# A spectral layer beside a routed expert layer: the inverse row transform on f32, and work between the engines dealt out anew

## The chip, the cores and the metric

The kernel runs on one core of one Trainium2 chip. The metric is the device time of one launch in microseconds; the whole kernel is one launch. A time comes with the span of the profile, from the core's first instruction to its last, which is some 2 us shorter.

## The reference

The input is normalised row by row; two layers work on the result, and both are added to the input. Cut to what matters:

```python
S, D = 2048, 576            # rows, columns
x  = A_x
xn = layernorm(x)           # no learned scale
# A: a filter in the frequency plane
X = rfft2(xn) * (w_r + 1j * w_i)        # 2048 x 289
a = irfft2(X, (S, D))
# B: for each row and each of 32 heads, one expert of 64
q  = einsum("nd,dhc->nhc", xn, w_q)     # c = 2 * 128
s1 = q[..., :128] @ k1.T                # 8 scores
s2 = q[..., 128:] @ k2.T                # 8 scores
e  = 8 * argmax(s1) + argmax(s2)        # the softmax over one candidate is 1
b  = sum over heads of gelu(xn . u[e]) * v[e]
out = x + a + b
```

## The kernel before, in words

**Layer A** is a two-dimensional Fourier transform made of matrix products. The 2048 rows are 16 tiles of 128. `ln` takes mean and variance of some tiles; the standard deviation's inverse lies in `rr[:, 0]`, and `rr[:, 2]` is -4 times the mean. `folds(t)` adds and subtracts mirrored halves of a row tile, twice, so that a transform of 576 needs short products; the result is `F`, and `Rs` is the first transform's matrix scaled by the row's `rr`. `dft128(t)` multiplies them: a transform over 64 rows. Its result lies in `AB` as f32 (a view, `AF_`) and in `ABL` (33 leftover frequencies, as f16 high and low halves). For three of the 16 tiles (`RTS`) the products are cut into halves of 64 array rows.

Then 16 steps `g` each hold 128 rows of the frequency plane: `d_fwd(g)` is the forward row transform on f32 (products named `c,AB`), `s_fwd` the column transform, `s_mul` multiplies with the filter (`Wt`), `s_inv` is the inverse column transform. `s_inv` writes its result back into `AB`, as an f16 high half (ScalarE) and an f16 low half, the difference (VectorE). Last come the 16 row tiles `t`: `d_inv(t)` is the inverse row transform, three f16 products (high by high, high by low, low by high) for each of four pieces, an eviction with the inverse scale `sc[:, 12:13]`, and folds on VectorE and GpSimd; `fin(t)` turns the result back over 64 rows with the matrix `RT`, adds layer B's products with `v` in the same PSUM bank, adds the input and stores.

**Layer B** never makes `q`: the keys are folded into `w_q` (`fold_part`, `fold_end`, `fold_last`), as differences from the first key of eight, so that each of the 64 (head, side) pairs has 7 score columns of 448 in `MU` and `MUL`; 64 more columns are `u`. `x_t` loads the transposed input and splits it into two f16 halves. `scores(r)` (8 times, 256 rows each) multiplies them: 28 products of 512 columns each, named `MU,xT` and `MUL,xT`. After it VectorE finds the maximum over a pair's 7 columns (`mx`), flags who equals it (`w<-banks,mx`) and weights the flags with a power of two of the key's number (`w<-w,wt`). `route(r)` reduces these to an expert's code and `combine(r)` to the 64 experts' weights, which GpSimd and TensorE turn (`CZ`) for `fin`.

**The order.** The program is first recorded as a list of operations, with their dependencies. `issue` then runs a planner (`forward`): a model of the five engines that takes, whenever an engine is free, the ready operation with the best place in the table `RANK`. So the table and the model's costs set the order on every engine, and which PSUM banks are used. Each engine works its list in order. All instructions come out of one helper line, so the profile is read by the names of tiles.

Of the kernel before, what the change touches and what calls it, by code (L numbers as in the profile page):

```python
# [32 lines left out]
def _consts():  # L33
# [13 lines left out]
    place = np.arange(16).reshape(4, 4).T.ravel()  # L47
# [48 lines left out]
    C1[[0, 144, 288]] *= 0.5  # L96
    C1 = np.where((j <= 144)[:, None] == ev[None, :], C1, 0)
# [12 lines left out]
    ic = np.zeros((128, 2, 2, 290), np.float16)  # L110
# [6 lines left out]
    for b, m in enumerate((_clean(CI) * 64, _clean(SI) * 64)):  # L117
        hi, lo = _hl(m)
        for q, h in enumerate((hi, lo)):
            ce = slice(0, 145) if b == 0 else slice(145, 290)  # L120
            co = slice(145, 290) if b == 0 else slice(0, 145)
            ic[:, b, q, ce] = h[:128, ce]
            ic[:, b, q, co] = h[161:, co]
        il[:99, b] = np.concatenate([hi[128:161], hi[128:161], lo[128:161]])
    c16 = np.concatenate([dl.reshape(128, -1), ic.reshape(128, -1), il.reshape(128, -1)], 1)
    c16 = np.concatenate([dc.reshape(128, -1), c16.view(np.float32)], 1)
# [164 lines left out]
class _Plan:  # L291
# [7 lines left out]
    def cost(self, eng, m, out, ins, kw):  # L299
# [6 lines left out]
        if eng == "tensor":  # L306
# [3 lines left out]
            if kw.get("tile_position"):  # L310
                q = _parts(ins[0])
                return c * q[0] * q[1] / 16384, 230.0
# [222 lines left out]
def _body(ctx, tc, nc, plan, a, out):  # L535
# [366 lines left out]


    XT, gate = {}, set()

    @staged
    def x_t(r):

# [343 lines left out]
```

## Time and profile before

| | |
|---|---|
| time of the runs, us | 223.46, 222.16, 222.97; median 222.97 |
| the profiled execution: time, span | 221.33 us, 219.5 us |
| busy, us | PE 193.5, DVE 178.0, ACT 132.5, POOL 134.1 |
| granted TensorE clock | 0.995 |
| read, written | 43.0 MB, 4.7 MB |

PE is TensorE's products, PEld its weight loads, DVE VectorE, ACT ScalarE, POOL GpSimd. A row of a group gives its line, engine, operation, what it writes and reads, shapes and number of instructions; then the busy time in us and the mean duration in ns; then the idle time of the engine just before them and what ended it. The ends of products are modelled; their starts are not, so a product's price is the distance between starts. A product on f32 leaves two records.

### The profile page before, as it was taken

To read this page: it belongs to the slowest core of one execution; us is meant where nothing else is said; L and a number is where in the kernel's file an instruction comes from. 1 tells how busy PE (TensorE), PEld (TensorE's weight loads), DVE (VectorE), ACT (ScalarE), POOL (GpSimd) and SP (SyncE) were. 2 spreads that over 40 slices of the span, in tenths; PEclk is the share of its full clock that TensorE was granted. 3 is DMA by queue.
4 is the path that set the end of the run, shared out by engine and by line. 5 is a ranking of instruction groups with operands and counts; after the bars stand their busy time and mean duration, and the time that the engine had idled before them with its cause. 6 is when DMAs were issued, how large, how long until landed. Compare 5 with 4: busy or idle time off the path is not lost.

```text
span 219.5 us, 6058 instructions
## 1 busy us (share of the span) xinstructions
PE 193.5 (88%) x2360; PEld 130.7 (60%) x2360; DVE 178.0 (81%) x417; ACT 132.5 (60%) x285; POOL 134.1 (61%) x179
## 2 busy tenths in 40 slices
PE   0197899999999989999989999999979999998690
PEld 0175576679568546764657545655547787477560
DVE  1989899854646777763999999998899999999980
ACT  2268787979946977988595983855832333043220
POOL 4776787515189307394767963947734985667560
PEclk9999999999999999999999999999999999999998
DMA  6999999999999999993362404201100136204376
GB/s 198 380 417 418 422 418 423 395 403 400 366 383 356 405 408 423 437 345 133 103 199 63 131 0 122 73 3 24 39 0 3 28 87 162 54 0 108 96 176 165
DMA packets 17020, 48.12 MB, mean 219 GB/s; under 512 B 2144, under 2 KB 8544, under 8 KB 16224
## 3 DMA queue, kind: packets, MB, share of 16 engines
q1 hardware_dynamic: 16992, 47.74, 60.6%
q8 instruction: 18, 0.29, 0.5%
q14 instruction: 10, 0.08, 0.1%
HBM read 43.01 MB, written 4.72 MB: 217 GB/s over the span
## 4 chain that ended last, share of the span: by engine, by line
PE 50%; DVE 33%; ACT 6%; issue 5%; DMA 2%; POOL 1%; ACTq 0%; DVEq 0%; POOLq 0%
PE banks L523 50%; DVE MT L523 8%; DVE t L523 7%; DVE w L523 5%; DVE XN L523 3%; DVE AB L523 2%; DVE mx L523 2%; DVE st L523 2%; DMA XN<-in_x_dram 2%; DVE A L523 2%; DVE ABL L523 2%; ACT t L523 1%; ACT ABL L523 1%; ACT AB L523 1%; ACT Rs L523 1%
## 5 line engine op out<-in xcount | busy, mean ns | idle before, releaser
L523 PE MATMUL banks<-MU,xT 128*128 128x512 f16 x192 | 45.5, 379 | 0.4 <-DVE t L523 0.4
L523 POOL TENSOR_TENSOR A<-t 128x145 f32<-128x145 f32 (+2 forms) x48 | 32.3, 688 | 14.1 <-DVE t L523 11.6
L523 PE MATMUL banks<-c,AB 128*128 128x145 f16 (+2 forms) x320 | 38.2, 253 | 1.0 <-DVE AB L523 1.0
L523 POOL TENSOR_TENSOR y<-t,t 128x289 f32<-128x289 f32 x32 | 23.0, 742 | 20.9 <-DVE t L523 20.5
L523 PEld LDWEIGHTS <-xT 128*128 128x128 f16 x224 | 20.9, 98 | 23.9 <-issue 0.9
L523 POOL TENSOR_TENSOR xT<-xf,xT 128x640 f16<-128x640 f32 x16 | 22.4, 1403 | 18.2 <-ACT xf L523 18.1
L523 DVE SCALAR_TENSOR_TENSOR t<-banks,wx,Wt 128x578 f32<-128x578 f32 x32 | 24.4, 810 | 4.1 <-PE banks L523 4.0
L523 ACT ACTIVATE yh<-banks,sc 128x580 f32<-128x580 f32 (+1 forms) x16 | 10.0, 627 | 25.1 <-PE banks L523 24.0
L523 POOL TENSOR_TENSOR yh<-y,yh 128x578 f16<-128x578 f32 x16 | 21.8, 1377 | 4.7 <-issue 2.7
L523 ACT ACTIVATE AB<-banks 128x512 f32<-128x512 f32 (+1 forms) x32 | 18.7, 592 | 5.5 <-PE banks L523 2.9
L523 PE MATMUL banks<-Rs,yl 128*99 128x128 f32 (+1 forms) x76 | 10.3, 290 | 12.6 <-ACT Rs L523 12.1
L523 PE MATMUL banks<-w,KP 128*32 128x288 f32 x256 | 20.4, 420 | 0.6 <-DMA w<-in_wq_dram 0.4
L523 PE MATMUL banks<-c,ABL 99*128 99x289 f16 (+1 forms) x64 | 18.6, 295 | 2.4 <-DVE XN L523 1.4
L523 DVE TENSOR_TENSOR ABL<-banks,ABL 33x256 f16<-33x256 f32 x32 | 12.9, 407 | 8.8 <-ACT ABL L523 6.2
L523 POOL TENSOR_TENSOR t<-XN 128x289 f32<-128x289 f32 x20 | 15.8, 799 | 5.3 <-DMA XN<-in_x_dram 2.5
L523 PEld LDWEIGHTS banks<-c,AB 128*128 128x128 f32 x128 | 18.0, 191 | 1.5 <-DVE AB L523 0.9
L523 PEld LDWEIGHTS <-AB 128*128 128x128 f16 x192 | 17.2, 146 | 2.5 <-issue 1.6
L523 PE MATMUL banks<-Rs,A 128*128 128x128 f32 (+1 forms) x152 | 18.0, 291 | 0.4 <-ACT Rs L523 0.4
L523 DVE TENSOR_REDUCE MT<-w 128x128 bf16<-128x896 bf16 (+1 forms) x16 | 18.3, 1141 | 0.1
L523 PEld LDWEIGHTS banks<-Rs,A 128*128 128x128 f32 (+1 forms) x152 | 16.8, 205 | 2.0 <-ACT Rs L523 1.0
L523 PE MATMUL banks<-A,s 64*64 64x289 f32 x256 | 17.8, 410 | 0.0
L523 PEld LDWEIGHTS banks<-Rs,yl 128*99 128x99 f32 (+1 forms) x76 | 8.1, 177 | 15.8 <-ACT Rs L523 13.5
(126 smaller groups left out, 409.1 us busy)
## 6 DMA issues: line engine op xcount, KB each, us to landing
w<-in_wq_dram SPq DMA_DIRECT2D x32, 576.0 KB, 7.4
xf<-in_xT_dram SPq DMA_DIRECT2D x16, 320.0 KB, 3.9
Wt<-in_W_dram SPq DMA_DIRECT2D x8, 578.0 KB, 6.9
out_dram<-XN SPq DMA_DIRECT2D x32, 144.0 KB, 2.4
XN<-in_x_dram SPq DMA_DIRECT2D x3, 1154.0 KB, 10.2
s<-in_s_dram SPq DMA_DIRECT2D x16, 192.0 KB, 4.2
XN<-in_xd_dram SPq DMA_DIRECT2D x2, 1152.0 KB, 8.9
XN<-in_xd_dram SPq DMA_DIRECT2D x1, 2304.0 KB, 12.9
```

The costliest lines, as they stand in the source:

```text
L523: fn(*[x.place() if isinstance(x, _Ps) else x for x in args], **{k: x.place() if isinstance(x, _Ps) else x for k, x in kw.items()})
```

## The change

- The inverse row transform takes f32: `s_inv` writes one f32 result with ScalarE, VectorE's subtraction of 512 elements falls away, `d_inv` has one f32 product in the place of three f16 ones, and the constants `ic` are f32 (as many bytes).
- The inverse scale goes into the last transform's constants: `RT` is multiplied with it once. The evictions of `d_inv` then have no pointer to a scale, and VectorE's are plain adds and subtracts. In the same way `cst` takes the scale of `combine`.
- The score columns lie key by key (64 pairs for each of 7 keys) instead of pair by pair. The flags of score tiles 0 to 6 are weighted by seven ScalarE instructions of 128 elements each, and `combine`'s two casts to integers go to ScalarE.
- A constant column is zeroed in the forward constants, so the folds need no mean: a plain add takes the place of the one with `rr[:, 2]`, and the step that made it goes.
- Of the second folds, GpSimd gives eight to VectorE (`DF`). Of the 16 input splits, six (`XL`) go from ScalarE and GpSimd to one VectorE instruction each.
- `RTS` goes: all 16 first transforms are whole. The table that turns the Gelu on is loaded by an instruction of its own (`gelu_table`).
- The planner's costs differ, and `RANK` is another table.

```diff
-    1200, 1203, 1204, 1217, 1230, 1244, 1205, 1236, 588, 595, 828, 589, 1117, 799, 1029, 1035, 319, 1118, 965,
+    769, 771, 812, 1250, 1253, 1279, 757, 802, 305, 871, 417, 306, 842, 1217, 951, 1061, 935, 1086, 981, 983,
...
+    C1[:, ll == 0] = 0.0
...
-        for q, h in enumerate((hi, lo)):
...
-            ic[:, b, q, ce] = h[:128, ce]
-            ic[:, b, q, co] = h[161:, co]
+        ic[:, b, ce] = m[:128, ce]
+        ic[:, b, co] = m[161:, co]
...
-ABt = AB.rearrange("p q c (n t) -> p q c n t", t=16)
+ABt = AF_.rearrange("p c (n t) -> p c n t", t=16)
...
-    RTS = (9,10,11,)
+    DF = (0,2,4,6,8,10,12,14,)
...
-        G.tensor_tensor(F[:, 1, 0:145], e[:, 1, 0:145], e[:, 1, 288:143:-1], op=OP.add)
-        V.scalar_tensor_tensor(F[:, 0, 0:145], e[:, 0, 0:145], rr[:, 2, t:t + 1], e[:, 0, 288:143:-1],
-                               op0=OP.add, op1=OP.add)
+        (V if t in DF else G).tensor_tensor(F[:, 1, 0:145], e[:, 1, 0:145], e[:, 1, 288:143:-1], op=OP.add)
+        V.tensor_tensor(F[:, 0, 0:145], e[:, 0, 0:145], e[:, 0, 288:143:-1], op=OP.add)
...
+        V.tensor_scalar(RT, RT, sc[:, 12:13], None, op0=OP.mult)
...
+            if 2 * r + i in XL:
+                V.scalar_tensor_tensor(v, w, bx[:, 3:4], h, op0=OP.mult, op1=OP.subtract)
+                continue
...
-        V.tensor_tensor(wk[:, 896:1792].rearrange("p (t n) -> p t n", t=2), wk[:, 0:896].rearrange("p (t n) -> p t n", t=2),
-                        wt.unsqueeze(1).to_broadcast([128, 2, 448]), op=OP.mult)
+        if r in AW:
+            for e in range(7):
+                A.activation(we[:, :, e], eq[:, :, e], AF.Copy, scale=2.0 ** -(6 * e + 6 + 6 * (e > 2)))
+        else:
+            V.tensor_tensor(we, eq, wt.unsqueeze(1).to_broadcast([128, 2, 7, 64]), op=OP.mult)
...
-            V.tensor_scalar(ci[:, :, w], cw[:, w].rearrange("p t i -> p (t i)"), 2.0 ** (18 + 30 * w), None, op0=OP.mult)
+            A.activation(ci[:, :, w], cw[:, w].rearrange("p t i -> p (t i)"), AF.Copy, scale=2.0 ** (18 + 30 * w))
...
-        A.activation(hi, pv, AF.Copy)
-        V.tensor_tensor(ab, pv, hi, op=OP.subtract)
+        A.activation(ABz[:, :, z, :], pv, AF.Copy)
...
-                for n, (ha, hb) in enumerate(((0, 0), (0, 1), (1, 0))):
-                    P.matmul(p[:, b, cs], ABt[:, ha, 2 * c + b, :, t], ic[:, b, hb, cs], start=False,
-                             stop=(c == 1 and n == 2))
+                P.matmul(p[:, b, cs], ABt[:, 2 * c + b, :, t], ic[:, b, cs], start=False, stop=(c == 1))
...
-        V.scalar_tensor_tensor(eo[:, :, 0:145], p[:, :, 0:145], sc[:, 12:13], qs, op0=OP.mult, op1=OP.add)
+        V.tensor_tensor(eo[:, :, 0:145], p[:, :, 0:145], qs, op=OP.add)
```

Three places of the order. The first is VectorE where the inverse row transforms are under way and the last score tile (`mx_130`, `w_123`) comes; `XN` is the addition to the input of one finished row tile, `t` an eviction of `d_inv`, `MT` are the small tiles of `route` and `combine`. Before:

```order
L523 SCALAR_TENSOR_TENSOR t_1_99<-banks,sc,yh_134 128x2x145
L523 TENSOR_REDUCE MT<-w_122 128x32
L523 SCALAR_TENSOR_TENSOR MT<-MT,sc 128x128
L523 TENSOR_REDUCE mx_130<-banks 128x128
L523 TENSOR_TENSOR MT<-MT,fm 128x128
L523 TENSOR_TENSOR w_123<-banks,mx_130 128x896
L523 SCALAR_TENSOR_TENSOR XN<-banks,sc,XN 128x576
L523 SCALAR_TENSOR_TENSOR t_0_98<-banks,sc,yh_133 128x2x145
L523 TENSOR_TENSOR w_123<-w_123,wt 128x896
L523 SCALAR_TENSOR_TENSOR MT<-MT,sc 128x128
L523 SCALAR_TENSOR_TENSOR t_1_99<-banks,sc,yh_134 128x2x144
L523 SCALAR_TENSOR_TENSOR t_1_99<-banks,sc,yh_134 128x2x145
```

Now:

```order
L527 TENSOR_REDUCE mx_130<-banks 128x128
L527 TENSOR_TENSOR t_0_98<-banks,yh_133 128x2x145
L527 SCALAR_TENSOR_TENSOR XN<-banks,sc,XN 128x576
L527 TENSOR_TENSOR w_123<-banks,mx_130 128x896
L527 SCALAR_TENSOR_TENSOR XN<-banks,sc,XN 128x576
L527 TENSOR_TENSOR w_123<-w_123,wt 128x896
L527 TENSOR_TENSOR t_1_99<-banks,yh_134 128x2x145
L527 TENSOR_TENSOR t_1_99<-banks,yh_134 128x2x144
L527 TENSOR_REDUCE MT<-w_123 128x128
L527 TENSOR_TENSOR t_0_98<-banks,yh_133 128x2x145
L527 SCALAR_TENSOR_TENSOR XN<-banks,sc,XN 128x576
L527 SCALAR_TENSOR_TENSOR MT<-mx_130,MT 128x128
```

Before, six of the 16 row tiles' additions stand ahead of the last score tile's maximum (five of them above these rows), and now none: the score tiles have moved ahead of the inverse row transforms.

The second place is ScalarE in the score tiles, where it evicts PSUM (`A<-banks` is `d_fwd`, `AB<-banks` is `s_inv`), splits the input (`xT`, `xf`) and takes Gelus (`MT<-banks,gs`). Before:

```order
L523 ACTIVATE xf_124<-xf_124,bx 128x640
L523 ACTIVATE MT<-banks,gs 128x64
L523 ACTIVATE xT_94<-xf_125,bx 128x640
L523 ACTIVATE xf_125<-xf_125,bx 128x640
L523 ACTIVATE AB<-banks 128x8x64
L523 ACTIVATE ABL<-banks 99x4x64
L523 ACTIVATE t_0_108,wm<-Wt_112 128x1156
```

Now:

```order
L527 ACTIVATE yl_106<-yh_133 128x396
L527 ACTIVATE xT_94<-xf_125,bx 128x640
L527 ACTIVATE w_121<-w_121 128x2x64 x7
L527 ACTIVATE xT_95<-xf_126,bx 128x640
L527 ACTIVATE MT<-banks,gs 128x64
L527 ACTIVATE A_1_101<-banks 128x578
L527 ACTIVATE xT_95<-xf_124,bx 128x640
L527 ACTIVATE MT<-MT 128x16
```

Seven weightings of one score tile's flags stand in a row ahead of the next eviction; a copy `xf` is gone, since VectorE splits that tile, and a cast to integers has come.

The third place is the start of the queue of loads on SP: `XN` are the blocks of x, `c_68` the first constants, `w` the weights of the fold, `s` and `Wt` column matrices and filter. Before:

```order
L523 DMA XN<-in_x_dram 128x1154
L523 DMA s_1_116<-in_s_dram 128x384
L523 DMA s_3_118<-in_s_dram 128x384
L523 DMA c_68<-in_c_dram 128x320
L523 DMA XN<-in_x_dram 128x1154
L523 DMA kT<-in_kT_dram 128x16
L523 DMA s_2_117<-in_s_dram 128x384
L523 DMA s_0_115<-in_s_dram 128x384
L523 DMA XN<-in_x_dram 128x2308
L523 DMA w_119<-in_wq_dram 128x1152
L523 DMA XN<-in_x_dram 128x2308
```

Now:

```order
L527 DMA kT<-in_kT_dram 128x16
L527 DMA XN<-in_x_dram 128x1154
L527 DMA c_68<-in_c_dram 128x320
L527 DMA mk<-in_mk_dram 128x99
L527 DMA XN<-in_x_dram 128x1154
L527 DMA s_0_115<-in_s_dram 128x384
L527 DMA XN<-in_x_dram 128x2308
L527 DMA w_120<-in_wq_dram 128x1152
L527 DMA Wt_112<-in_W_dram 128x1156
L527 DMA XN<-in_x_dram 128x2308
```

The constants `s` that stood between the blocks of x have moved behind, the small `kT` has moved to the front, and a filter block stands ahead of the last block but one.

More of the change, by code (lines that the diff above doesn't have):

```diff
@@ L45, in _consts @@
     R = _clean(R)
-    place = np.arange(16).reshape(4, 4).T.ravel()
+    place = np.arange(16) // 2 + 8 * (np.arange(16) % 2)
     F = np.zeros((2, 64, 16, 2, 2, 2))
@@ L757, in dft128 @@
         for b in range(2):
-            P.matmul(p[:99, 1, 128 * b:128 * b + 128].rearrange("p (q i x) -> p i q x", i=2, x=8), FL[:, b, :, :].rearrange("p a b -> p (a b)"), Rs, start=True, stop=True)
-        A.activation(hi, m, AF.Copy)
+            P.matmul(p[:99, 1, 128 * b:128 * b + 128], FL[:, b, :, :].rearrange("p a b -> p (a b)"), Rs, start=True, stop=True)
+        A.activation(AF_.rearrange("p c (h n) -> p (c h) n", n=64)[:, :, 4 * t:4 * t + 4], m, AF.Copy)
+        lo = ABL[:99].rearrange("p b (h n) -> p (b h) n", n=64)[:, :, 4 * t:4 * t + 4]
         A.activation(lo, l, AF.Copy)
@@ L895, in fold_last @@
             turned(p[:, c], c, 3)
-        m = MU[:, :, :, 336:448].rearrange("p h c (m e) -> p h c m e", e=7)
-        parted(m[:, 0], m[:, 1], p[:, :, :, :7], 1)
+        m = MU[:, :, :, :448].rearrange("p h c (e m) -> p h c e m", m=64)[:, :, :, :, 48:64]
+        q = p.rearrange("p c m e -> p c e m")[:, :, :7]
+        A.activation(m[:, 0], q, AF.Copy, scale=sc[:, 7:8])
+        for c in range(4):
+            V.scalar_tensor_tensor(m[:, 1, c], q[:, c], sc[:, 7:8], m[:, 0, c], op0=OP.mult, op1=OP.subtract)
         p = PS("m", (128, 16, 8))
         turned(p, 4, 3)
-        m = MUL[:, :, 336:448].rearrange("p h (m e) -> p h m e", e=7)
-        parted(m[:, 0], m[:, 1], p[:, :, :7], 1, 64)
+        m = MUL[:, :, :448].rearrange("p h (e m) -> p h e m", m=64)[:, :, :, 48:64]
+        parted(m[:, 0], m[:, 1], p.rearrange("p m e -> p e m")[:, :7], 1, 64)
     XT, gate = {}, set()
+    XL = (4,5,6,7,8,9,)
     @staged
@@ L1005, in d_fwd @@
                 cs = slice(0, 145) if b == c else slice(145, 289)
-                P.matmul(p[:, b, cs], ABg[:, 2 * b + c, g // 4, g % 4, :], dc[:, b, cs], start=False, stop=(c == 1))
+                P.matmul(p[:, b, cs], ABg[:, 2 * b + c, g // 2, g % 2, :], dc[:, b, cs], start=False, stop=(c == 1))
         A2[g] = T([128, 2, L], F32, "A2", 2)
@@ L1099, in d_inv @@
             es = T([128, 2, 290], F32, "qs", 2, "yh")
-            A.activation(es, p[:, :, 0:290], AF.Copy, scale=sc[:, 12:13])
+            A.activation(es, p[:, :, 0:290], AF.Copy)
             qs = es[:, :, 145:290]
```

98 lines of the change are left out of this document (43 added, 55 removed), and 124 rows, old and new, of the table RANK.

## The prediction

> **What bounds the kernel now.** I read first the busy time of the engines by stage. I cut the span where the work changes kind: loading; layer norm, folds and the first transform; the column transforms with the weights being folded; the same with the scores; the inverse row transforms and the output; the last store. The numbers are the stage's length, then busy time (and instructions) of PE, PEld, DVE, ACT and POOL, the granted clock, the DMA share and the rate.
>
> ```profile
> 0.00:10.00 10.00, 0.05 (x1) 0.05 (x1) 5.47 (x24) 2.74 (x6) 5.55 (x17) 1.00 0.81 273
> 10.00:49.60 39.60, 36.04 (x358) 27.39 (x358) 33.93 (x115) 31.23 (x85) 25.66 (x44) 1.00 1.02 415
> 49.60:103.20 53.60, 52.60 (x676) 35.38 (x676) 32.38 (x80) 43.67 (x85) 28.61 (x30) 1.00 0.96 373
> 103.20:163.70 60.50, 58.75 (x691) 34.11 (x688) 56.41 (x103) 40.13 (x79) 40.82 (x42) 1.00 0.24 69
> 163.70:213.70 50.00, 46.05 (x644) 33.80 (x644) 49.05 (x98) 14.70 (x33) 33.48 (x48) 1.00 0.32 77
> 213.70:219.50 5.80, 0.00 (x0) 0.00 (x0) 0.79 (x1) 0.00 (x0) 0.00 (x0) 0.82 0.71 170
> ```
>
> From 10 us on, TensorE idles 3.56, 1.00, 1.75 and 3.95 us in the four working stages. VectorE fills the last of them to 49.05 of 50.00 us, and the one before to 56.41 of 60.50. So two engines are full at once, TensorE throughout and VectorE from 103 us on. The chain of waits agrees: long stretches on TensorE alone, and VectorE for the rest.
>
> ```profile
> PE 50%; DVE 33%; ACT 6%; issue 5%; DMA 2%; POOL 1%; ACTq 0%; DVEq 0%; POOLq 0%
> ```
>
> ```profile
> 78.34 30.53 PE banks L523 x374
> ```
>
> Then I asked what TensorE waits for: first in the inverse stage, then in the first-transform stage (total us, times, longest; the 10.0 of the last row is the wait for the very first input).
>
> ```profile
> PE banks L523 <- DVE XN L523: 2.0, 4, 1.1
> PE banks L523 <- DVE t L523: 1.1, 2, 0.7
> PE banks L523 <- DVE ABL L523: 0.9, 1, 0.9
> PE banks L523 <- DVE AB L523: 0.5, 1, 0.5
> PE banks L523 <- POOL A L523: 0.2, 1, 0.2
> ...
> PE banks L523 <- ACT Rs L523: 12.6, 4, 10.0
> ```
>
> In the inverse stage all waits but 0.2 us are for VectorE. That is what the change relieves. It cannot return more than TensorE now waits, and whatever it adds to TensorE is paid in full.
>
> **The change part by part.** *Inverse row transform on f32.* Per row tile and half, two products on f32 replace six on f16. Their prices are read from starts, since the ends are modelled; the forward transform already has the f32 shape.
>
> ```profile
> 85.50 0.66 PE L523 MATMUL banks<-c,AB 128*128 128x145 f32 x4
> 85.99 0.29 PE L523 MATMUL banks<-c,ABL 99*128 99x289 f16 x1
> 86.12 0.66 PE L523 MATMUL banks<-c,AB 128*128 128x144 f32 x4
> 86.70 0.45 PE L523 MATMUL banks<-w,KP 128*32 128x288 f32 x4
> ...
> 192.39 0.56 PE L523 MATMUL banks<-c,AB 128*128 128x145 f16 x6
> 192.79 0.29 PE L523 MATMUL banks<-c,ABL 99*128 99x290 f16 x1
> ```
>
> Four f32 records, two products, take 85.50 to 85.99, or 0.245 us a product. Six f16 products take 192.39 to 192.79, or 0.067 each, and three of them 0.20. So the 64 products cost TensorE 64 x (0.245 - 0.20) = +2.9 us, with nothing to hide them. Between 86.12 and 86.70 lie 0.58 us for four records, 0.09 more than above: the price of a change of the array's shape. The new order has 102 such changes for 98, +0.4 us. The three row-tiled first transforms that go cost about what the plain ones cost: 0. TensorE: +3.3 us.
>
> The inverse weights are read with a step of 16 elements, 64 bytes on f32, and no f32 load here has a step. The nearest rows are the f16 load with a step and the f32 load without.
>
> ```profile
> L523 PEld LDWEIGHTS <-AB 128*128 128x128 f16 x192 | 17.2, 146 | 2.5 <-issue 1.6 <-DVE AB L523 0.6
> L523 PEld LDWEIGHTS banks<-c,AB 128*128 128x128 f32 x128 | 18.0, 191 | 1.5 <-DVE AB L523 0.9
> ```
>
> Stepped loads of 146 ns already start every 67 ns, so 79 ns of one lie under its neighbour. An f32 load of 191 less 79 needs 112 ns, under the 122 ns of an f32 record: hidden, +0. If the step makes it half as long again (287), it needs some 208 and shows by 86 ns on 128 loads: +11 us. I take 0, since the f32 row is the nearer one, and keep 11 as the end.
>
> Of a load of 128 columns the Trainium skill (TensorE: Matmul & The Clock Gate, LDWEIGHTS) says that it takes the columns over 1.2 GHz, 107 ns, an estimate by which it would stay hidden as well. The page says nothing there of a step, and no run here shows a stepped f32 load.
>
> *VectorE in the inverse stage.* Its rows in that stage, and the score products that TensorE runs there:
>
> ```profile
> L523 DVE TENSOR_REDUCE MT<-w 128x32 f32<-128x1024 bf16 x5 | 6.0, 1206 | 0.0
> L523 DVE TENSOR_TENSOR w<-w,MT 128x512 bf16<-128x512 bf16 x10 | 4.6, 485 | 0.0
> L523 DVE TENSOR_SCALAR MT<-MT 128x16 int32<-128x16 f32 x10 | 2.4, 263 | 0.0
> L523 DVE TENSOR_REDUCE mx<-banks 128x128 f32<-128x896 f32 x2 | 2.1, 1074 | 0.0
> L523 DVE TENSOR_TENSOR w<-banks,mx 128x896 bf16<-128x896 f32 x2 | 2.1, 1074 | 0.0
> L523 DVE TENSOR_TENSOR w<-w,wt 128x896 bf16<-128x896 bf16 x3 | 1.9, 624 | 0.0
> ...
> L523 PE MATMUL banks<-MU,xT 128*128 128x512 f16 x36 | 8.6, 379 | 0.4 <-DVE t L523 0.4
> ```
>
> In the new order two of these five sums are left there, four of the ten products, none of the ten integer casts (ScalarE has them), one maximum and one comparison of two, and one weighting of three: 3.6 + 2.8 + 2.4 + 1.1 + 1.1 + 1.2 = 12.2 us. The smaller pieces of the same score tiles give some 3 more. The 24 evictions without a pointer to a scale give 24 x 0.06 = 1.5: the row with it is 506 ns, and the plain reads of PSUM below (407 for 256 elements, 678 for 512) put 290 elements at 443. VectorE falls from 49 to about 32 us. Most of this is moved, not saved: 36 of the 44 score products, some 8 us of TensorE, now stand ahead of the first inverse transform. TensorE needs 46.05 - 8 + 3.3 = 41.4 us here, so VectorE has 9 us to spare and the wait for it should mostly go. I take -3.0 of 3.95. Ends: -3.95, and 0 if other waits fill the room.
>
> *VectorE before that.* All 16 subtractions of the column transform's result go, seven of eight weightings, and six input splits come to it. The rows for these and for the terms further down:
>
> ```profile
> L523 DVE TENSOR_TENSOR AB<-banks,AB 128x512 f16<-128x512 f32 x16 | 10.8, 678 | 2.0 <-ACT AB L523 2.0
> L523 DVE TENSOR_TENSOR ABL<-banks,ABL 33x256 f16<-33x256 f32 x32 | 12.9, 407 | 8.8 <-ACT ABL L523 6.2 <-ACT AB L523 2.6
> L523 DVE SCALAR_TENSOR_TENSOR t<-banks,sc,yh 128x290 f32<-128x290 f32 x16 | 8.1, 506 | 0.0
> L523 DVE SCALAR_TENSOR_TENSOR A<-t,rr 128x145 f32<-128x145 f32 x16 | 7.1, 448 | 0.9 <-POOL t L523 0.7
> L523 DVE TENSOR_TENSOR A<-t 128x288 f32<-128x288 f32 x16 | 7.2, 448 | 0.0
> L523 DVE SCALAR_TENSOR_TENSOR vS<-Wt,sc,vS 128x576 f16<-128x576 f32 x1 | 0.8, 819 | 0.3 <-ACT vS L523 0.3
> L523 POOL TENSOR_TENSOR A<-t 128x145 f32<-128x145 f32 x16 | 8.5, 535 | 6.3 <-DVE t L523 4.1 <-PE banks L523 1.0 <-ACT Rs L523 0.9
> L523 POOL TENSOR_TENSOR xT<-xf,xT 128x640 f16<-128x640 f32 x16 | 22.4, 1403 | 18.2 <-ACT xf L523 18.1
> L523 ACT ACTIVATE xf<-xf,bx 128x640 f32<-128x640 f32 x16 | 13.2, 823 | 0.2
> L523 ACT ACTIVATE CZ<-MT 128x128 f16<-128x128 f32 x8 | 2.5, 308 | 5.6 <-DVE MT L523 5.6
> ```
>
> In the score stage VectorE loses nine subtractions (6.1), its weightings (3.1) and casts (1.6); it gains what was moved forward (some 12.3) and three splits (near the 819 row, 0.9 each: 2.7). That is 56.4 + 4.2, or 61 of a stage that grows to 68 us. TensorE waits 1.75 us there, and I leave that: 0, between -1.75 and +3. The column stage idles 1.0 us; without the subtraction between eviction and next use, -0.3.
>
> *ScalarE.* 49 weightings of 128 elements, near the 308 ns row, are 15.1 us, and 16 small casts some 4; six of the 823 ns copies go, 4.9, and GpSimd is relieved of six splits of 1403 ns. In the score stage ScalarE comes to 40.1 + 15 + 3 - 2.5 = 56 of 68 us. It has room, so I cost this at 0. But it evicts PSUM in the same queue: up to 2.2 us of weightings, seven in a row, can stand ahead of an eviction that TensorE waits for. That is a rival below.
>
> A rule of the Trainium skill speaks against this part: ScalarE: Activation LUTs, Rules for kernel authors, has multiplication on VectorE, up to three times faster in bf16. The trace agrees on the price, 624 ns for one weighting against 7 x 308 = 2156; by this rule the change loses wherever ScalarE is waited for.
>
> *First transform.* The mean is no longer folded in, so 16 fused adds of 448 ns become plain adds. The row with 288 plain elements is 448, and its share for 145 is 226; I take 300, so -2.4 us. Eight folds come from GpSimd, +2.4. VectorE: 0 (ends -3.5 and 0). GpSimd loses 8 x 0.535 = 4.3 us of 25.66, and the step that scaled the mean. The loads are reordered: ahead of the end of the second and third block of x stand 1.40 and 2.78 MB for 1.74 and 3.32. At the stage's 415 GB/s they land 0.8 and 1.3 us earlier; the first block, behind a load of 8 KB, hardly later. TensorE idles 3.56 us here, 2.6 of it for Rs, which comes after that chain. I take -2.0 (ends -3.56 and +0.5).
>
> **Sum:** +3.3 - 3.0 - 0.3 - 2.0 = -2.0 us. The profiled execution took 221.33 us, 219.5 of span and 1.8 around it, so 219.3. The median of the runs is 222.97, 1.6 above that execution, and on its scale I predict 221.0. The bound between change and none is 0.5%, 1.1 us, about what a measurement of this kernel can tell.
>
> **The rivals**, on the median's scale.
>
> *The waits go altogether.* TensorE's idle time of all four stages, 10.26 us, shrinks to 3: +3.3 - 7.3 = -4.0, and 1 us of waits shorter than a matmul's modelled end comes on top: 218. With all of it gone and that 1 us: 215.0. For it: VectorE, which most waits name, is relieved. Against it: in the first-transform stage, where much of the idle time lies, VectorE has as much work as before.
>
> *Slower: the filler is gone.* In the inverse stage before, score products filled TensorE while a tile went from its transform through ScalarE, VectorE and GpSimd to the last product. Now 8 of 44 are left, and GpSimd, 33.48 us of 50 before, has the same work in 42, 80%. If its adds become the last thing waited for, the stage idles 7 us in place of 3.95: +3.3 + 3 - 0.3 - 1.5 = +4.5, or 227.5. It decides as soon as the inverse stage gives back less than 1 us: already then +3.3 - 1 - 1 makes 224.3. For it: TensorE has the least room of all engines. Against it: only 0.2 us of today's waits name GpSimd.
>
> *ScalarE comes late.* If half of the seven weighting blocks each hold an eviction for 2.2 us, +7.7 on the forecast: 228.7. For it: 56 of 68 us are taken. Against it: no wait of TensorE in that stage names ScalarE today. The rule of ScalarE: Activation LUTs named above points this way.
>
> *The stepped f32 load shows:* +11 at most, 232; half of it, 226.5.
>
> **How the numbers follow.** Forecast (219 to 223.5) 0.46; waits gone 0.18; filler gone 0.21; ScalarE late 0.08; load 0.07. Faster by over 0.5%, below 221.9: 0.18 and three quarters of 0.46, together 0.52. Same: 0.10 of the forecast and 0.04 of the filler's mild end, 0.14. Slower: 0.34. Below 215.5 I leave some 0.04, above 228 some 0.14, of the last two rivals and the worst of the filler. The likeliest case's own range is 219 to 223.5.
>
> **What would show it.** Right: 128 f32 records of the inverse at a pitch near 122 ns; no subtraction named AB; VectorE under 36 us and TensorE's idle time under 1.5 in the inverse stage, which is 41 to 43 us long; a score stage near 68; the first-transform stage near 37.6. Wrong: a pitch over 140 (load); waits of TensorE for GpSimd of over 1 us in the inverse stage (filler); waits for ScalarE of over 2 us in the score stage; a first-transform stage no shorter than 39.6, which takes the 2.0 away and leaves the time near 223.

## The result, and the profile after

The changed kernel takes 237.62 us, median of 4 runs (237.20 to 238.09), beside 222.56 for the kernel before (4 runs, 221.69 to 223.46): a ratio of 1.068, 95% interval 1.062 to 1.073. It is slower by 15 us, and outside the predicted range. The profiled execution took 238.09 us with a span of 236.3, 16.8 more span than before.

The busy time by stage, cut at the same events as before: first transform, first product of the column transforms, first maximum over scores, first inverse product, last product. Columns as in the prediction.

```profile
0.00:10.30 10.30, 0.00 (x0) 0.00 (x0) 5.08 (x24) 2.62 (x6) 5.20 (x19) 1.00 0.78 262
10.30:51.00 40.70, 36.43 (x309) 28.33 (x310) 36.91 (x125) 34.30 (x90) 19.80 (x29) 0.96 0.99 386
51.00:106.20 55.20, 54.49 (x684) 36.03 (x684) 31.09 (x77) 38.59 (x76) 25.52 (x27) 1.00 0.97 376
106.20:177.50 71.30, 67.01 (x735) 37.52 (x733) 65.13 (x109) 49.46 (x138) 36.63 (x40) 1.00 0.20 58
177.50:229.30 51.80, 51.80 (x536) 44.32 (x536) 35.95 (x63) 13.07 (x37) 30.14 (x46) 1.00 0.30 72
229.30:236.30 7.00, 0.08 (x3) 0.00 (x0) 0.82 (x1) 0.00 (x0) 0.00 (x0) 0.78 0.64 155
```

Against the six rows of before, the stages grow by 0.3, 1.1, 1.6, 10.8, 1.8 and 1.2 us. The score stage has taken over some 8 us of score products from the inverse stage, so only some 3 of its 10.8 are a loss; and the inverse stage, which gave those 8 us away and has lost every wait for VectorE (TensorE is busy 51.80 of 51.80 us, VectorE only 35.95), is not 8 us shorter but 1.8 longer. That is where to look. The chain of waits, by engine, now stands on TensorE:

```profile
PE 59%; DVE 22%; ACT 5%; DMA 5%; issue 5%; POOL 1%; SPq 0%; POOLq 0%; ACTq 0%; DVEq 0%
```

The groups of weight loads in the inverse stage, and one row tile of it on TensorE's timeline (start, length, tile, count):

```profile
L527 PEld LDWEIGHTS banks<-c,AB 128*128 128x128 f32 x128 | 30.8, 311 | 0.4 <-issue 0.2
```

```profile
195.91 0.34 PE L527 MATMUL banks<-c,ABL 99*128 99x290 f16 x1
196.09 1.02 PE L527 MATMUL banks<-c,AB 128*128 128x145 f32 x4
196.95 0.29 PE L527 MATMUL banks<-c,ABL 99*128 99x290 f16 x1
197.08 1.03 PE L527 MATMUL banks<-c,AB 128*128 128x145 f32 x4
```

Four f32 records take from 196.09 to 196.95, 0.215 us each, where the prediction had 0.122; a load takes 311 ns, where it had 191 and put the danger at 287. The 128 records so cost 128 x 0.093 = 11.9 us more than forecast. It is the small rival, *the stepped f32 load shows*, with a chance of 0.07 and a worst case of +11.

In the score stage VectorE is busy 65.13 of 71.30 us. Its groups there, costliest first, have one that was at 1074 ns before:

```profile
L527 DVE TENSOR_REDUCE MT<-w 128x128 bf16<-128x896 bf16 x6 | 10.3, 1709 | 0.6 <-ACT w L527 0.6
```

This is the maximum over the seven weighted flags of a pair. With scores key by key, the seven lie 64 elements apart.

In the first-transform stage the granted clock is 0.96. One of the span's 40 slices stands at 0.7: from 25.1 to 28.5 us the clock is at half, 0.50. On the timeline the same 16 records take 3.54 us there and 1.95 outside:

```profile
PEclk9999799999999999999999999999999999999997
```

```profile
23.41 0.68 PE L527 MATMUL banks<-Rs,yl 128*99 128x128 f32 x4 [1.04 <-ACT Rs L527]
24.59 0.76 PE L527 MATMUL banks<-Rs,yl 128*99 128x128 f32 x4 [0.50 <-ACT Rs L527]
25.14 3.54 PE L527 MATMUL banks<-Rs,A 128*128 128x128 f32 x16
28.62 0.69 PE L527 MATMUL banks<-w,KP 128*32 128x288 f32 x8
29.24 1.12 PE L527 MATMUL banks<-Rs,yl 128*99 128x128 f32 x8
30.19 1.95 PE L527 MATMUL banks<-Rs,A 128*128 128x128 f32 x16
```

So there were three suspects: the step of the f32 load, the maximum over flags that lie apart, and the clock. The rival to all three was the new order, in which little work beside the inverse is left.

### The profile page after: what moved, and what is told of

It is laid out like the page before. It is cut to its first block, busy times and chain, and to the rows that moved or that the text cites. A ratio compares the mean times of both kernels' runs of the same rounds, so it can differ in the third digit from the quotient of the medians.

```text
span 236.3 us, 5862 instructions
## 1 busy us (share of the span) xinstructions
PE 209.8 (89%) x2260; PEld 146.2 (62%) x2260; DVE 175.0 (74%) x397; ACT 138.0 (58%) x345; POOL 117.3 (50%) x160
## 4 chain that ended last, share of the span: by engine, by line
PE 59%; DVE 22%; ACT 5%; DMA 5%; issue 5%; POOL 1%; SPq 0%; POOLq 0%; ACTq 0%; DVEq 0%
PE banks L527 59%; DVE MT L527 6%; DVE t L527 4%; DVE w L527 3%; DMA w<-in_wq_dram 3%; DVE st L527 2%; DVE A L527 2%; DVE mx L527 2%; DMA XN<-in_x_dram 2%; POOL y L527 1%; DVE ABL L527 1%; ACT MT L527 1%; DVE rr L527 1%; ACT t L527 1%; ACT yl L527 1%
## 5 line engine op out<-in xcount | busy, mean ns | idle before, releaser
L527 PE MATMUL banks<-c,AB 128*128 128x145 f32 (+1 forms) x256 | 53.2, 334 | 0.0
L527 PEld LDWEIGHTS banks<-c,AB 128*128 128x128 f32 x256 | 48.9, 250 | 2.2 <-issue 1.4
L527 POOL TENSOR_TENSOR A<-t 128x289 f32<-128x289 f32 (+2 forms) x40 | 25.6, 657 | 10.6 <-DVE t L527 9.3
L527 ACT ACTIVATE yh<-banks 128x580 f32<-128x580 f32 (+1 forms) x16 | 8.5, 533 | 30.0 <-PE banks L527 25.8
L527 POOL TENSOR_TENSOR xT<-xf,xT 128x640 f16<-128x640 f32 x10 | 14.0, 1404 | 18.8 <-ACT xf L527 18.7
L527 PE MATMUL banks<-Rs,yl 128*99 128x128 f32 x64 | 10.5, 306 | 14.2 <-ACT yl L527 10.3
L527 ACT ACTIVATE AB<-banks 128x512 f32<-128x512 f32 x32 | 18.6, 592 | 6.3 <-PE banks L527 5.6
L527 DVE TENSOR_TENSOR t<-banks,yh 128x290 f32<-128x290 f32 (+1 forms) x24 | 10.3, 456 | 14.9 <-ACT yh L527 12.9
L527 PE MATMUL banks<-Rs,A 128*128 128x128 f32 x128 | 19.0, 308 | 0.0
L527 PEld LDWEIGHTS banks<-Rs,A 128*128 128x128 f32 x128 | 18.1, 223 | 0.9 <-issue 0.9
```

The source lines that it names most:

```text
L527: fn(*[x.place() if isinstance(x, _Ps) else x for x in args], **{k: x.place() if isinstance(x, _Ps) else x for k, x in kw.items()})
```

## The experiments

Each is the changed kernel with one edit, unless it says otherwise. In the runs with more or fewer instructions the order of all others was written out as it had been; only where a new order is named, in the text or in the expectation, was one made. The expectations cut the stages at rounder times: their 73.5 for the score stage, from 104 us on, is the 71.30 above.

**The inverse's weights without a step.**

```diff
+        wc = T([128, 4, 128], F32, "wc", 3, "xf")
+        A.activation(wc, ABt[:, :, :, t], AF.Copy)
...
-                P.matmul(p[:, b, cs], ABt[:, 2 * c + b, :, t], ic[:, b, cs], start=False, stop=(c == 1))
+                P.matmul(p[:, b, cs], wc[:, 2 * c + b], ic[:, b, cs], start=False, stop=(c == 1))
```

> ScalarE copies the four weight blocks of a row tile side by side before the inverse transform loads them, so that its f32 weights are read without a step; 16 copies are added and the order from the first of them on is set anew around them. Theory S (the step of the f32 load sets the pace of the inverse): the 128 f32 records start every 125 ns instead of about 217, the inverse stage falls from 51.7 to some 40 us, and the time from 237.6 to 225 to 227. Rival O (the order: too little work beside the inverse): the pitch may fall, but the time stays within 2 us of 237.6. Rival W (f32 weights at this size, stepped or not): pitch stays above 200 ns, time 237 or more, the copies being on top.

Measured: 228.23 us (226.80 to 228.68), ratio to the kernel before 1.023 (1.016 to 1.029), 9.4 us under the changed kernel. The loads, four records of the inverse, and the score and inverse stages:

```profile
L529 PEld LDWEIGHTS banks<-c,xf 128*128 128x128 f32 x128 | 18.8, 195 | 0.8 <-issue 0.3 <-ACT xf L529 0.3
```

```profile
195.74 0.66 PE L529 MATMUL banks<-c,xf 128*128 128x145 f32 x4
196.24 0.29 PE L529 MATMUL banks<-c,ABL 99*128 99x290 f16 x1
```

```profile
105.80:177.00 71.20, 66.91 (x735) 37.48 (x732) 65.09 (x109) 49.93 (x138) 36.70 (x40) 1.00 0.19 58
177.00:219.60 42.60, 41.80 (x537) 32.82 (x536) 35.59 (x63) 27.55 (x53) 30.51 (x46) 1.00 0.37 88
```

The load is back at 195 ns, four records take 0.50 us (195.74 to 196.24) where they took 0.86, and the inverse stage is at 42.60 us, in the 41 to 43 that the prediction had set; the score stage has not moved. Theory S holds and rival W falls. Rival O's bound of 2 us is passed by far, though the order of this stage is a new one here too; the next run keeps the old one. The time is 1.2 us above the bound that I gave, since that had put the stage at some 40.

**Which steps cost.** The tiles read their weights at eight steps:

```diff
+    STEP, kept = (16, 1, 2, 3, 4, 6, 8, 12), []
...
-                P.matmul(p[:, b, cs], ABt[:, 2 * c + b, :, t], ic[:, b, cs], start=False, stop=(c == 1))
+                P.matmul(p[:, b, cs], AF_[:, 2 * c + b, 8 * (t % 2):8 * (t % 2) + 127 * u + 1:u], ic[:, b, cs], start=False, stop=(c == 1))
```

> The 16 inverse tiles read their f32 weights, from other places of the same tensor, at steps of 16, 1, 2, 3, 4, 6, 8 and 12 elements, two tiles each, 16 loads a step; the rest is unchanged, so the output is another one. Theory S: the load's time and the records' pitch depend on the step: 190 and 125 ns at step 1, 310 and 217 at step 16, and between them they rise with the step. If the cost is one of whether there is any step at all, 2 is as slow as 16. Rival W: the same pitch of over 200 ns at every step.

Measured: 234.26 us, a single run; two of the 16 tiles keep the step of 16. The group of these loads in the stretch of each pair of tiles; from the top, steps of 1, 2, 3, 4, 6, 8, 12 and 16 elements, 4 bytes each:

```profile
L528 PEld LDWEIGHTS banks<-c,AB 128*128 128x128 f32 x16 | 2.3, 193 | 0.1
L528 PEld LDWEIGHTS banks<-c,AB 128*128 128x128 f32 x16 | 2.3, 198 | 0.0
L528 PEld LDWEIGHTS banks<-c,AB 128*128 128x128 f32 x16 | 3.2, 266 | 0.2 <-issue 0.2
L528 PEld LDWEIGHTS banks<-c,AB 128*128 128x128 f32 x16 | 4.1, 326 | 0.0
L528 PEld LDWEIGHTS banks<-c,AB 128*128 128x128 f32 x16 | 3.9, 314 | 0.0
L528 PEld LDWEIGHTS banks<-c,AB 128*128 128x128 f32 x16 | 4.2, 334 | 0.0
L528 PEld LDWEIGHTS banks<-c,AB 128*128 128x128 f32 x16 | 4.6, 363 | 0.0
L528 PEld LDWEIGHTS banks<-c,AB 128*128 128x128 f32 x16 | 3.8, 309 | 0.1
```

A step of 8 bytes costs 5 ns, 12 bytes cost 73, and from 16 bytes on the load takes 310 to 360 ns with no further rise in order. The median distance between the starts of the records follows: 126, 126, 173, 233, 222, 238, 266 and 217 ns. It is the size of the step, and not "any step". Every engine works the same list here as in the changed kernel, so its order is not the cause. The Trainium skill (Advanced Engine Details and Errata, SBUF Cachelines) says that SBUF has lines of 16 bytes and that fewer than two accesses to a line cost time. The trace agrees at every step: two f32 elements to a line at step 2, fewer at 3, one from 4 on. That rule spoke against this change, and the prediction did not weigh it.

**The maximum over flags that lie side by side.** First only its reading was changed, so that it takes the maximum of other flags:

```diff
-        wv = wk[:, 896:1792].rearrange("p (t e m) -> p t m e", t=2, e=7)
+        wv = wk[:, 896:1792].rearrange("p (t m e) -> p t m e", t=2, e=7)
```

> The maximum over the weighted flags reads seven neighbours in place of the seven keys 64 apart, in the same order of all instructions; it so takes other flags, and the output is another one. Nothing is moved to another engine. Theory F (VectorE paces the score stage, and this maximum is the part of the change that it pays for): the maximum falls from 1.72 to about 1.08 us, the score stage from 73.5 to about 69.5, the time from 237.6 to 233 to 234. Rival (TensorE paces that stage, or the order alone): time within 1 us of 237.6.

Measured: 234.33 us (233.30 to 234.82), ratio 1.052 (1.047 to 1.057): 3.3 us less. The maximum, and the stage:

```profile
L527 DVE TENSOR_REDUCE MT<-w 128x128 bf16<-128x896 bf16 x6 | 6.5, 1076 | 0.6 <-ACT w L527 0.6
```

```profile
106.10:174.80 68.70, 66.31 (x734) 37.52 (x732) 61.68 (x109) 49.48 (x139) 36.38 (x40) 1.00 0.20 60
```

VectorE loses 3.5 us of the stage and the stage 2.6, to the 68 us that were predicted for it. Theory F holds, a little weaker than the 3.6 to 4.6 expected of it.

Then two ways to have that for real. The first lets the weightings write pair by pair:

```diff
-        eq, we = (wk[:, 896 * k:896 * k + 896].rearrange("p (t e m) -> p t e m", t=2, e=7) for k in range(2))
+        eq = wk[:, 0:896].rearrange("p (t e m) -> p t e m", t=2, e=7)
+        we = wk[:, 896:1792].rearrange("p (t m e) -> p t e m", t=2, e=7)
```

> Only the weighted flags are written pair by pair again, seven keys side by side, by the same instructions; scores and flags stay key by key. Theory F (VectorE paces the score stage, and the maximum over the seven keys pays for reading them 64 apart): that maximum falls from 1.71 to about 1.07 us, the score stage from 73.5 to about 69.5, the time from 237.6 to 233 to 234. Rival: the ScalarE weightings pay for the scattered writes what VectorE gains, or TensorE is what paces the stage: time within 1 us of 237.6.

Measured: 250.28 us (249.04 to 250.99), ratio 1.121 (1.113 to 1.130): 13 us more than the changed kernel. The weightings of ScalarE (298 ns in the changed kernel), the one that is left on VectorE, and the maximum:

```profile
L527 ACT ACTIVATE w<-w 128x128 bf16<-128x128 bf16 x49 | 27.8, 855 | 0.5 <-DVE w L527 0.4
L527 DVE TENSOR_TENSOR w<-w,wt 128x896 bf16<-128x896 bf16 x1 | 3.7, 3693 | 0.0
L527 DVE TENSOR_REDUCE MT<-w 128x128 bf16<-128x896 bf16 x8 | 8.7, 1083 | 7.1 <-ACT w L527 5.8 <-ACT MT L527 1.1
```

The maximum is as quick as hoped, and VectorE waits 7.1 us ahead of it, 5.8 of them for weightings that take three times as long. Two-byte elements written 14 bytes apart make them 2.9 times as long on ScalarE and 6 times on VectorE (615 ns in the changed kernel); reading them 128 bytes apart made the maximum 1.6 times as long. The rival had the mechanism; neither expectation had the time. Some of the 13 us is clock: it falls to half for 3.4 us twice in the score stage.

The second takes the maximum in three element-by-element steps:

```diff
-        V.tensor_reduce(v0.rearrange("p (t m) -> p t m", t=2), wv, axis=AX, op=OP.max)
+        V.tensor_tensor(wv[:, :, 3:6], wv[:, :, 0:3], wv[:, :, 3:6], op=OP.max)
+        V.tensor_tensor(wv[:, :, 3:5], wv[:, :, 3:5], wv[:, :, 5:7], op=OP.max)
+        V.tensor_tensor(v0.rearrange("p (t m) -> p t m", t=2), wv[:, :, 3], wv[:, :, 4], op=OP.max)
```

> In the changed kernel the maximum over seven keys is taken in three element-by-element maxima of 384, 256 and 128 flags, each reading what lies side by side; same place in the order. Theory F: about 0.35 + 0.28 + 0.22 = 0.85 us in place of 1.72, VectorE 7 us less, the score stage some 4 to 5 shorter, the time 232.5 to 234. Rival (TensorE or the order paces the stage): within 1 us of 237.6.

Measured: 238.10 us (237.03 to 239.68), ratio 1.069 (1.062 to 1.076): nothing gained. The time is the rival's, though not its reason: the run in which only the reading was changed shows that the stage does follow this maximum.

```profile
L529 DVE TENSOR_TENSOR MT<-w 128x128 bf16<-128x128 bf16 x8 | 4.9, 606 | 0.3
L529 DVE TENSOR_TENSOR w<-w 128x384 bf16<-128x384 bf16 x8 | 3.8, 473 | 1.3 <-ACT w L529 1.3
L529 DVE TENSOR_TENSOR w<-w 128x256 bf16<-128x256 bf16 x8 | 3.2, 401 | 0.3
```

The three take 606 + 473 + 401 = 1480 ns, not 850. The shortest single ones are near the estimate; one of 128 elements takes from 224 to 1449 ns. The Trainium skill (SBUF — State Buffer, Who interferes with whom) has an instruction of VectorE with two inputs in SBUF contend with one of GpSimd that reads SBUF; these maxima have two, the reduction has one. The trace agrees: of the eight of 128 elements, the four beside which GpSimd does nothing take 224 to 226 ns, and the four beside which it works 598 to 1449. What GpSimd does beside the longest, the longest, and a short one:

```profile
128.24 1.41 POOL L529 TENSOR_TENSOR xT<-xf,xT 128x640 f16<-128x640 f32 x1 [1.17 <-ACT xf L529]
128.27 1.45 DVE L529 TENSOR_TENSOR MT<-w 128x128 bf16<-128x128 bf16 x1
...
131.61 0.22 DVE L529 TENSOR_TENSOR MT<-w 128x128 bf16<-128x128 bf16 x1
```

No run here took GpSimd's work away, so so the cause is read from this coincidence alone.

**Scores pair by pair, weightings on VectorE.** The first try undid the order of the scores but left the splits of the keys in their new loops, and the weightings became one instruction on VectorE:

```diff
-        if r in AW:
-            for e in range(7):
-                A.activation(we[:, :, e], eq[:, :, e], AF.Copy, scale=2.0 ** -(6 * e + 6 + 6 * (e > 2)))
-        else:
-            V.tensor_tensor(we, eq, wt.unsqueeze(1).to_broadcast([128, 2, 7, 64]), op=OP.mult)
+        V.tensor_tensor(we, eq, wt.unsqueeze(1).to_broadcast([128, 2, 64, 7]), op=OP.mult)
```

> Scores, flags and weighted flags lie pair by pair again, and all eight weightings are on VectorE, one instruction each; all else keeps its place in the order. Theory F: VectorE loses 8 x 0.64 us in the maximum and gains 7 x 0.67 in weightings, so it is as busy as in the changed kernel, and the time stays within 1.5 us of 237.6, though ScalarE is relieved of 49 weightings (14 us). Rival A (ScalarE is late because of the weightings): the time falls by 3 us or more.

Measured: 246.04 us (245.84 to 248.14), ratio 1.107 (1.101 to 1.113). It tells nothing of the weightings: the key splits now wrote two-byte elements 14 bytes apart, 1631 ns each where the changed kernel has 534, and the first score product came 6.6 us later (102.5 us for 95.9). So it was done again with those loops as they were before:

```diff
-        parted(m[:, 0], m[:, 1], p.rearrange("p b m e -> p e (b m)")[:, :7], 0, 128 if c < 4 else 64)
+        parted(m[:, 0], m[:, 1], p.rearrange("p b m e -> p (b m) e")[:, :, :7], 0, 128 if c < 4 else 64)
```

> As the run with scores pair by pair, but the folded keys are also written in the order of the kernel before, pair by pair in rows of seven, so that the splits of the keys write side by side. Theory F: VectorE has 8 x 0.64 less in the maximum and 7 x 0.67 more in weightings: within 1.5 us of 237.6, with ScalarE 14 us less busy. Rival A (ScalarE's weightings hold evictions up): 3 us faster or more. If it is slower by 8 us again, the scattered writes of the key splits were not the cause of that run's loss.

Measured: 240.40 us (238.46 to 241.84), ratio 1.078 (1.071 to 1.086): slower than the changed kernel by 2.8, on neither theory's side.

```profile
L526 DVE TENSOR_REDUCE MT<-w 128x128 bf16<-128x896 bf16 x8 | 8.6, 1072 | 0.0
L526 DVE TENSOR_TENSOR w<-w,wt 128x896 bf16<-128x896 bf16 x8 | 6.5, 808 | 0.2
```

```profile
104.60:179.50 74.90, 68.54 (x734) 37.77 (x733) 69.12 (x117) 40.18 (x90) 36.97 (x40) 0.98 0.18 55
```

VectorE is 4.0 us busier in the score stage, and the stage 3.6 longer. The weighting takes 808 ns there, not the 670 of my sum: six of the eight take 615 to 624 ns, the other two 1220 and 1512, both beside GpSimd's work. And the clock, 0.98 of 74.90, took some 1.5 us of the stage; how much of the 3.6 is left for VectorE was not settled. In the total the clock does not tell the two traces apart, since the changed kernel has such a drop in its first stage and this one has none there. What the run does show: taking ScalarE's 49 weightings away makes nothing faster. The rule of the Trainium skill that the prediction named (ScalarE: Activation LUTs, Rules for kernel authors) does hold for the price, 808 ns on VectorE for 7 x 298 on ScalarE; it doesn't decide here, since VectorE is the engine that paces the stage.

**TensorE kept busy in the first stage.**

```diff
-            for q in range(4):
+            for k in range(4 * FILL.get((b, s), 1)):
+                q = k % 4
...
+    mt, FILL = {}, {(0, 0): 3, (0, 2): 2}
```

> The changed kernel, in which TensorE multiplies the first part of the folded weights three times and the third part twice, in the two stretches of the first-transform stage where it sat idle (1.6 us at 16 us, 1.0 and 0.5 at 22 to 24.6); so the sums, and with them the output, are others. Theory C (the clock drops because TensorE idles there, and that is the stage's loss): no slice of the stage under full clock, the column transforms begin at some 49.3 us in place of 50.9, the time 1 to 2 us below 237.6. Rival (layer norm and folds on VectorE pace the stage, the drop hides behind them): the drop may go, the column transforms still begin at 50.5 or later, and the time stays.

Measured: 236.51 us (236.26 to 236.54), ratio 1.061 (1.055 to 1.067): 1.1 us less, and every run below those of the changed kernel.

```profile
PEclk9999999999999999999999999999999999999998
```

```profile
10.40:50.20 39.80, 37.33 (x357) 27.81 (x358) 36.17 (x125) 34.40 (x90) 19.69 (x29) 1.00 1.01 401
```

No slice of the stage is below full clock, and the stage takes 39.80 us for 40.70. Theory C holds for 0.9 to 1.1 us; the column transforms begin at 50.2, between the two expectations.

But this drop is not the change's own. In the run below that puts three parts of the change into the kernel before, and keeps its order, the clock is at half from 18.9 to 22.3 us. And of the 21 runs of the kernel before that stand beside this one, the ten with a granted clock of 0.990 or less took 222.7 to 224.3 us, the eleven with 0.993 or more 221.1 to 222.3. The profile that the stages of before were read from, with 0.995, is one of the latter kind. So the filling took away a loss that both kernels have in part of their executions, and it explains little of the 15 us between their medians.

**All three at once**: the gathered weights, the maximum over neighbours and the filling, in the order of the gathered run.

> The gathered weights of the inverse, the maximum over neighbours and the filled stretches of the first stage in one kernel; as in those runs the filling and the maximum make another output. If the three causes are separate, their gains add: 237.6 less 9.4, 3.3 and 1.1 makes 223.8, so 222.5 to 225, and what the change costs beyond them is 1 us or so. Rival: one engine paces after the other, so that a gain beside another is worth less: 226 or more.

Measured: 223.87 us (223.71 to 224.10, 12 runs), ratio 1.005 (1.003 to 1.008). The three gains add up to within 0.1 us, closer than the spread of the runs, 1 us and more, could promise. The score and the inverse stage:

```profile
105.40:174.30 68.90, 66.52 (x734) 37.67 (x733) 61.92 (x109) 49.86 (x138) 36.36 (x41) 1.00 0.20 60
174.30:216.10 41.80, 41.77 (x537) 32.58 (x535) 34.54 (x63) 27.49 (x53) 30.28 (x46) 1.00 0.38 90
```

The load's step and the spread flags, which are the change's own, make up 12.7 of its 15.1 us; the other 2.4 were not split further.

**Towards a faster kernel.** The gathered weights and the three maxima, in a new order:

> The gathered weights of the inverse and the three maxima together, with all instructions of the program put in a new order, found by shifting them in a model of the engines that was set to the durations of the traces. By the parts: 228.2 for the gathered weights, less 4 to 5 for the maxima, less up to 3 for the order: 221 to 224 if the order brings nothing, 218 to 221 if it does. Rival: what VectorE gives back in the score stage is taken up by TensorE's own work there, and it stays above 225.

Measured: 227.46 us (226.15 to 228.86), ratio 1.022 (1.017 to 1.027). That is the rival's time. The new order moved the first column product to 55.4 us, with TensorE idle for 6 us of the stage before it and a slice at a clock of 0.6: the start lost what the end may have won, and the three maxima, by the run above, had little to give. Next, three parts of the change in the kernel before, in its own order:

```diff
-            V.tensor_scalar(ci[:, :, w], cw[:, w].rearrange("p t i -> p (t i)"), 2.0 ** (18 + 30 * w), None, op0=OP.mult)
+            A.activation(ci[:, :, w], cw[:, w].rearrange("p t i -> p (t i)"), AF.Copy, scale=2.0 ** (18 + 30 * w))
...
+        V.tensor_scalar(cst, cst, sc[:, 9:10], None, op0=OP.mult)
+        V.tensor_scalar(RT, RT, sc[:, 12:13], None, op0=OP.mult)
...
-        V.scalar_tensor_tensor(eo[:, :, 0:145], p[:, :, 0:145], sc[:, 12:13], qs, op0=OP.mult, op1=OP.add)
+        V.tensor_tensor(eo[:, :, 0:145], p[:, :, 0:145], qs, op=OP.add)
```

> The kernel before, in its own order, with three parts of the change that take work off VectorE: the 16 casts to integers on ScalarE, and the scales of inverse and combination folded into constants. VectorE loses 16 x 0.3 + 24 x 0.05 + 8 x 0.12 = 7 us of its 178, nearly all from 103 us on. Theory V (VectorE paces the end of the kernel before): 1.5 to 3 us faster than 222.7. Rival (the casts' way over ScalarE and back costs each route what it saves): within 1 us of 222.7.

Measured: 221.96 us (12 runs, 220.72 to 223.51), ratio 0.998 (0.994 to 1.002): no change that can be told, which is the rival's outcome. VectorE's busy time went from 178.0 only to 177.5 us, since other groups took longer, these two among them:

```profile
L525 DVE TENSOR_TENSOR w<-w,MT 128x512 bf16<-128x512 bf16 x16 | 9.5, 624 | 0.0
L525 DVE TENSOR_TENSOR MT<-MT,fm 128x128 int32<-128x128 int32 x8 | 3.5, 433 | 0.0
```

In the kernel before these are 539 and 311 ns. Of the first group seven single instructions take over 600 ns, for four in the kernel before; all of them run beside GpSimd's work, and those without it take 405 to 416. And with a new order from the column transforms on:

> The same parts in the kernel before, with the instructions from the column transforms on put in a new order, found by shifting them in a model of the engines set to the durations of the traces. Theory V: what VectorE saves is used, 216 to 220. Rival (the order of the kernel before was already the best for TensorE, which is full): 220 or above, no better than the run in the old order.

Measured: 221.89 us (12 runs, 220.93 to 222.46), ratio 0.996 (0.993 to 0.999). It is the one version whose interval lies below the kernel before, by 0.4%, and no faster than the run in the old order: the rival's outcome, far from the 216 to 220 of theory V.

## Why the prediction was wrong

*The step that failed: "hidden, +0" for the stepped f32 load.* The load did not stay under the products: it took 311 ns for the 191 that I had assumed, and the records, set apart by it, measured +11.9 us (0.215 for 0.122 us, 128 times). The two rows that I had were read rightly; the choice between them was wrong. The f16 row with a step, 146 ns, held the answer: it has 32 bytes between elements, where the f32 load has 64, and costs half as much again as the f16 load without a step (98). I took "nearest" by type instead of by step. The end of +11 was right, and ought to have had far more than 0.07. The 107 ns that the prediction quotes for a load of 128 columns is not what an f32 load takes here either: 190 to 195 ns without a step. Taking the step away gave 9.4 us back and not 11.9; there the copies keep ScalarE busy 27.55 us of the stage for 13.07, and TensorE idles 0.80 us. The rest was not traced.

By stage, with some 8 us for the score products that moved, the span missed the forecast by 9.5 us in the inverse stage, 3.1 in the first-transform stage, 2.8 in the score stage, 1.9 in the column stage, 1.2 after the last product and 0.3 in the loading.

*VectorE in the inverse stage*: forecast under 36 us, 35.95 measured; TensorE's idle time forecast under 1.5, 0.00 measured. The waits went entirely, -3.95 for the -3.0 that I took. The stage's length of 41 to 43 us came as soon as the step was gone (42.60 and 41.80). *The price of the f32 product without a step* was right too: four records with 0.50 us in the gathered run are 0.125 each.

*VectorE in the score stage*: costed at 0 and a stage near 68. The maximum over the flags was carried over at its old price; key by key it takes 1.72 us, VectorE is busy 65.13 us for the 61 of my sum, and the stage takes 71.30. Without that 68.70 and 68.90. Missed: 3.3 us.

*The first transform, -2.0*: it came out at +1.1. About 1 us of that is the clock, which the profile of before happens not to show. Even without it the stage is 39.80, just over the 39.6 that I had named as wrong. The loads did as forecast: the second and third block of x landed 0.6 and 1.1 us earlier (0.8 and 1.3 in the prediction). But Rs for the second group of tiles was ready at 17.60 us, for 17.50 before: VectorE, busy 7.20 of the 7.30 us up to there, set the pace there, and not the data. So the term's step from earlier loads to an earlier Rs failed. TensorE waits 3.8 us for Rs in the stage (total, times, longest), in place of 2.6,

```profile
PE banks L527 <- ACT Rs L527: 3.8, 4, 1.6
```

and VectorE, whose change I had put at 0, is busy 36.91 us for 33.93. The fused adds did fall as estimated (298 for 448 ns), but the means of small statistics and whole folds rose:

```profile
L527 DVE TENSOR_TENSOR A<-t 128x145 f32<-128x145 f32 x21 | 5.9, 298 | 0.0
L527 DVE TENSOR_TENSOR t<-XN 128x289 f32<-128x289 f32 x9 | 4.5, 504 | 0.0
L527 DVE SCALAR_TENSOR_TENSOR rr<-rr 128x4 f32<-128x4 f32 x6 | 2.0, 334 | 0.0
```

Before, the last two were 443 and 151 ns. The rise is a few long ones: one fold of 1054 ns and two of the statistics, 771 and 652, all three beside GpSimd's work; the others take 408 to 454 and 140 to 148.

*The tail* had no term, and grew by 1.2 in this one execution: 7.0 us from the last product to the end. The run with TensorE kept busy has the same order there, and ends 6.1 us after its last product, near the 5.8 of before; so most of the 1.2 is not the change's. In the profiled execution a store issued at 228.16 us landed after 4.3 us, where the median is 2.4; why was not settled.

*The rivals.* No wait of TensorE names GpSimd, so the filler was not missed. Its waits for ScalarE in the score stage come to 1.9 us, from none before and just under the bound of 2:

```profile
PE banks L527 <- ACT A L527: 1.1, 1, 1.1
...
PE banks L527 <- ACT yh L527: 0.8, 1, 0.8
```

The column stage, forecast at -0.3, is 1.6 longer, but by work (TensorE 54.49 busy for 52.60) and not by waits: 144 of the fold's products (`w,KP`) stand in it for 128, sixteen that stood in the first-transform stage before. At 0.62 us for eight (28.62 to 29.24 above) they are 1.2 us, which the first-transform stage was spared.

Not settled: what sets off the drop of the clock. Eight of the fourteen traces have it in the first-transform stage, all with a gap of TensorE of 1.64 us or more; five without it have no gap over 1.60, but one has 2.36 us and no drop.

## What to carry to other kernels

A matrix product that is changed to a wider type keeps its number of elements, and doubles the bytes between them: look at how the stationary operand lies before its price is taken from a row without a step. When data is laid out anew for one reader, list every reader and writer of it and price each; here the one that was not listed gave back what the others had won. Relief for an engine is worth only the waits for it: these were 4 us, and any cost put on the full engine beside it, TensorE, is paid in whole. And a profile is one execution: before a difference between two of them is put down to the change, see whether the runs of one kernel differ by as much.

## What the hardware showed that I had not expected

- The f32 weight load of 128 columns: 193 and 198 ns at 4 and 8 bytes between elements, 266 at 12, 309 to 363 from 16 to 64 bytes.
- Two-byte elements written 14 bytes apart: 855 ns for 128 on ScalarE in place of 298, 3693 for 896 on VectorE in place of some 620; reading two-byte elements 128 bytes apart cost VectorE's maximum only 1720 for 1074.
- Work taken off VectorE does not leave its busy time by as much: some 7 us of instructions went, and 0.5 us of busy time. Two-operand instructions that take 224 or 624 ns alone took up to 1449 and 1512 beside GpSimd's work.
- The granted clock drops to half for 3.4 us at a time, in the middle of work, in some executions of a kernel and not in others; ten of 21 runs of the kernel before were some 1.7 us longer, at a lower mean clock. What sets it off stays open.
